# A hand-written order of 812 steps, searched anew: more matmuls on zeros ahead of the first transposes, and chunk 6 stored by SyncE

## The chip, the cores and the metric

The kernel runs on one core of a Trainium2 chip. The metric is the device time of the whole kernel in microseconds, the median of three runs. In the text TensorE is PE, VectorE is DVE, ScalarE is ACT, GpSimd is POOL and SyncE is SP, as in the profile; "PEld" is PE's weight load.

## What is computed

Linear attention with the feature map phi, and a feed-forward network with a product of two projections on its output:

```python
def phi(x):
    return np.where(x > 0, x, np.exp(x) - 1.0) + 1.0
q_p, k_p = (phi(q), phi(k))                    # q, k, v: (8 batches, 8 heads, 576, 64), f32
kv = np.einsum('bhsd,bhse->bhde', k_p, v)
z = np.sum(k_p, axis=2)
num = np.einsum('bhsd,bhde->bhse', q_p, kv)
den = np.einsum('bhsd,bhd->bhs', q_p, z)[..., None] + 1e-06
x = (num / den) ...                            # heads side by side: (4608, 512)
out = ((x @ w1) * (x @ w2) @ w3) @ w_out       # w1, w2: 512x1024; w3: 1024x1024; w_out: 1024x512
```

## The kernel before, in words

**Staging.** A batch has 576 rows: 512 of them make one chunk, and the 64 left over of all eight batches make a ninth chunk (number 8). The product w3 @ w_out is formed once (eight blocks of 128 rows), since the two matrices follow each other with nothing between them. Then for each batch: phi of k and q, the 64x64 state `kv` of each head, the numerator and denominator, the division, a transpose to `xt`, and for each chunk eight blocks `f` of the two projections, their product `ab`, and four output blocks `o`.

**The order.** Nothing is looped at run time. A string `ORDER` (L451 to L522) lists every step; the loop at L528 issues them one after the other, and each engine takes its own instructions in exactly that order. `GATES` (L523) adds six waits that hold loads back until another load has landed. A step is `name:arguments`; a letter at the end names the engine of a copy (`a` ACT, `v` DVE) or the queue of a transfer (`s` SP, `g` POOL).

The steps that the text speaks of:

- `const:i` (L94): memsets; `const:1` makes the identity `ident` for transposes, on POOL. `warm:n,i` (L110): n matmuls of 128x128 zeros that nothing reads.
- `l3` (L155), `lo` (L148), `lw` (L141): load the blocks of w3, w_out, w1 and w2 on POOL's queue, with a cast. `ld` (L117): 1 MB, or part of it, of one batch of q, k or v, into a pool of five buffers. `lr`, `lp` (L124, L132): the left-over rows of k, q or v of one batch or two.
- `w3t` (L352): eight transposes of a w3 block on PE; `w3c` (L359): its copy out of PSUM. `wa`, `wf` (L369, L378): the product with w_out; `wc` (L385): the copy into `wf_sb`.
- `x` (L164), `t` (L170), `m` (L177): phi of four heads (exp on ACT, max and add on DVE) and of a pair of heads (min on DVE). `xr`, `tr`, `mr` the same for the left-over rows.
- `v` (L216), `vr` (L222): the cast of v. `kv` (L230): the state of two heads, on PE; `kc`, `kh` (L246, L255): its copy out of PSUM.
- `qt` with `qc` (L262, L271), or `qd` (L277, an SP transfer): the transpose of q. `na` (L288): numerator and denominator, on PE; `nd` (L305): three DVE instructions that divide. `xp` with `xc` (L328, L337), or `xd` (L342, an SP transfer): the transpose into `xt`.
- `f` (L397), `fk` (L401): one block of a chunk in both projections, 8 matmuls; `fk` does part of the inner dimension. `ac` (L405): the copy of the first, on ACT; `ab` (L410): the product, on DVE. `o` (L415), `oc` (L422), `st` (L434): an output block, its copy, its store. `ol` (L439): the last output block, in two halves.

PSUM has four buffers for `f`, `o`, `qt`, `xp`, `w3t` and `warm` together (`mm_ps`, L61) and two for `kv`, `na` and `wa` (`at_ps`, L62). So the third `f` in a row starts only when the first one's `ac` and `ab` are done. `v` has one cast buffer (L66).

```python
    for s in ORDER.split():
        name, *args = s.split(":")
        made = steps[name](*(int(a) if a.isdigit() else a for a in (args[0].split(",") if args else ())))
        issued[s] = made
        if s in gates:
            tc.add_manual_dep(made.ins, issued[gates[s]].ins.name, ...)
```

Of the kernel before, what the change touches and what calls it, by code (L numbers as in the profile page):

```python
# [18 lines left out]
def kernel(  # L19
# [441 lines left out]
    kv:0,2 t:q,0,4,4 kc:0,0,1,1,a kh:0,2,1,a kv:0,3 kh:0,2,0,v ld:k,1,0,8,g m:q,0,4,2 na:0,0 kh:0,3,0,a
    w3t:6 kh:0,3,1,v m:q,0,4,3 na:0,1 nd:0,0 qt:0,2,2 ld:q,1,0,8,g w3t:7 w3c:6,v qc:0,2,2,a xp:0,0
    w3c:7,v wf:6 ld:v,1,0,4,g lr:k,1,s xc:0,0,a nd:0,1 lr:v,1,s ld:v,1,4,4,g na:0,3 xp:0,1 wc:6,v na:0,2
    wf:7 nd:0,3 xc:0,1,v nd:0,2 xp:0,3 fk:0,0,0,2 wc:7,v xc:0,3,a xp:0,2 xc:0,2,v fk:0,0,2,1 fk:0,0,3,1
    ac:0,0,a f:0,1 ab:0,0 xr:k,0,1 ac:0,1,a tr:k,0,1 mr:k,0,1 f:0,2 ab:0,1 ac:0,2,a f:0,5 ab:0,2 vr:1,v
    ac:0,5,a f:0,4 ab:0,5 ac:0,4,a t:k,1,0,4 x:k,1,4,4 f:0,6 t:k,1,4,4 x:k,1,0,4 ab:0,4 m:k,1,4,2
    ac:0,6,a f:0,7 m:k,1,0,0 m:k,1,0,1 ab:0,6 x:q,1,0,4 lp:k,1,s t:q,1,0,4 f:0,3 ac:0,7,a m:q,1,0,0
    ld:k,2,0,8,s m:q,1,0,1 v:1,0,4,a m:k,1,4,3 ab:0,7 ac:0,3,a kv:1,1 t:q,1,4,4 qt:1,0,2 x:q,1,4,4
    ab:0,3 kv:1,0 o:0,2 v:1,6,2,a kc:1,0,1,1,v lp:v,1,s m:q,1,4,3 qc:1,0,2,a m:q,1,4,2 kc:1,0,1,0,a
    v:1,4,2,a qt:1,2,2 oc:0,2,v na:1,1 ld:q,2,0,8,s kv:1,2 qc:1,2,2,a st:0,2,g nd:1,1 kv:1,3 o:0,3  # L470
    kh:1,2,1,a kh:1,3,0,a kh:1,3,1,v kh:1,2,0,v ld:v,2,0,8,s xp:1,1 x:k,2,0,4 t:k,2,4,4 na:1,2 na:1,0
    oc:0,3,v o:0,1 xr:k,1,2 nd:1,2 st:0,3,g x:k,2,4,4 ld:k,3,0,8,s nd:1,0 xc:1,1,a na:1,3 xp:1,2
    oc:0,1,a m:k,2,4,3 o:0,0 nd:1,3 xc:1,2,a st:0,1,g tr:k,1,2 vr:3,a t:k,2,0,4 xp:1,3 vr:2,a xp:1,0
    m:k,2,0,0 x:q,2,0,4 xc:1,3,v lp:k,2,s xc:1,0,v m:k,2,0,1 oc:0,0,a f:1,1 mr:k,1,2 x:q,2,4,4 m:k,2,4,2
    st:0,0,g t:q,2,0,4 ac:1,1,a m:q,2,0,0 f:1,4 m:q,2,0,1 ab:1,1 v:2,4,4,a t:q,2,4,4 ac:1,4,a f:1,0
    m:q,2,4,2 ld:q,3,0,8,s m:q,2,4,3 v:2,0,4,a ab:1,4 qd:2 ac:1,0,a kv:2,1 ab:1,0 kv:2,0 f:1,5 x:k,3,4,4
    t:k,3,0,4 t:k,3,4,4 ac:1,5,a f:1,2 x:k,3,0,4 ab:1,5 ac:1,2,a f:1,3 ab:1,2 ac:1,3,a kv:2,2 x:q,3,4,4
    tr:k,2,2 ld:v,3,0,8,s f:1,7 ab:1,3 xr:k,2,2 ac:1,7,a mr:k,2,2 lp:v,2,s f:1,6 ab:1,7 ac:1,6,a kv:2,3
    ab:1,6 o:1,3 ld:k,4,0,8,s kc:2,0,2,0,a kc:2,0,2,1,a m:k,3,4,2 m:k,3,0,1 m:k,3,4,3 m:k,3,0,0
    x:q,3,0,4 na:2,3 na:2,1 t:q,3,0,4 o:1,0 lp:q,0,s oc:1,3,a nd:2,1 v:3,4,4,a st:1,3,g nd:2,3 xp:2,1  # L480
    v:3,0,4,a o:1,1 m:q,3,0,1 ld:q,4,0,8,s xc:2,1,v oc:1,0,a m:q,3,0,0 t:q,3,4,4 st:1,0,g na:2,0
    m:q,3,4,2 oc:1,1,a na:2,2 m:q,3,4,3 xp:2,3 o:1,2 nd:2,0 st:1,1,g qd:3 x:k,4,0,4 nd:2,2 x:k,4,4,4
    t:k,4,4,4 xp:2,0 xp:2,2 xc:2,3,a kv:3,3 xc:2,0,v kv:3,2 xc:2,2,a oc:1,2,v kv:3,1 vr:4,a kv:3,0
    t:k,4,0,4 st:1,2,g f:2,0 kc:3,0,2,0,a m:k,4,0,0 vr:5,a m:k,4,0,1 kc:3,0,2,1,a m:k,4,4,3 ac:2,0,a
# [12 lines left out]
    kv:5,3 nar:0 kv:5,1 ab:4,6 f:3,6 kc:5,0,2,0,a m:k,6,4,3 vr:7,a kc:5,0,2,1,v m:k,6,4,2 ac:3,6,a
    m:k,6,0,0 m:k,6,0,1 na:5,2 ld:v,6,0,8,s f:3,1 ndr:0 nd:5,2 xdr:0 ac:3,1,a ab:3,6 na:5,0 na:5,1 f:4,7
    nd:5,0 nd:5,1 ac:4,7,a na:5,3 ab:3,1 ld:q,6,0,8,s f:4,4 nd:5,3 ld:k,7,0,8,s v:6,0,4,a ab:4,7 xd:5
    o:3,1 ac:4,4,a v:6,4,4,a ab:4,4 kv:6,1 oc:3,1,a o:3,0 st:3,1,g x:q,6,4,4 t:q,6,0,4 o:3,2 t:q,6,4,4  # L500
    oc:3,0,a m:q,6,4,3 x:q,6,0,4 m:q,6,4,2 st:3,0,g kv:6,0 oc:3,2,v kv:6,3 kv:6,2 x:k,7,0,4 ld:q,7,0,8,s
    m:q,6,0,0 o:3,3 st:3,2,g m:q,6,0,1 t:k,7,0,4 qd:6 kc:6,0,2,0,a kc:6,0,2,1,a x:k,7,4,4 m:k,7,0,1
    m:k,7,0,0 f:4,1 oc:3,3,v t:k,7,4,4 st:3,3,g ac:4,1,a m:k,7,4,2 f:4,2 m:k,7,4,3 ab:4,1 ac:4,2,a
    ab:4,2 f:5,5 ac:5,5,a o:4,0 ab:5,5 f:5,2 oc:4,0,v x:q,7,4,4 lp:q,1,s t:q,7,4,4 st:4,0,g ac:5,2,a
    t:q,7,0,4 x:q,7,0,4 f:5,3 ab:5,2 ac:5,3,a f:5,4 ab:5,3 ac:5,4,a m:q,7,0,1 lp:q,2,s m:q,7,4,3 na:6,3
    m:q,7,0,0 na:6,1 ab:5,4 o:4,1 lp:q,3,s nd:6,1 m:q,7,4,2 ld:v,7,0,8,s nd:6,3 f:5,0 qd:7 oc:4,1,v
    ac:5,0,a st:4,1,g na:6,0 o:4,2 ab:5,0 nd:6,0 o:4,3 oc:4,2,a st:4,2,g na:6,2 v:7,0,4,a f:5,7 tr:q,1,2
    nd:6,2 oc:4,3,a v:7,4,4,a xd:6 st:4,3,g kv:7,1 kv:7,0 ac:5,7,a f:5,1 xr:q,1,2 ab:5,7 ac:5,1,a
    mr:q,1,2 xr:q,2,2 tr:q,2,2 kv:7,3 ab:5,1 kv:7,2 f:5,6 kc:7,0,2,1,a kc:7,0,2,0,v qdr:1 mr:q,2,2
    ac:5,6,a tr:q,3,2 xr:q,3,2 na:7,3 qdr:2 na:7,0 ab:5,6 o:5,0 nd:7,0 nd:7,3 o:5,1 oc:5,0,a st:5,0,g  # L510
    f:6,1 oc:5,1,a st:5,1,g ac:6,1,a f:6,0 ab:6,1 ac:6,0,a na:7,1 f:6,3 ab:6,0 nd:7,1 ac:6,3,a o:5,3
    mr:q,3,2 ab:6,3 nar:5 oc:5,3,a nar:4 f:6,6 ndr:5 st:5,3,g ndr:4 ac:6,6,a nar:2 xdr:2 na:7,2 ab:6,6
    f:6,7 nd:7,2 ac:6,7,a ndr:2 xd:7 f:6,4 ab:6,7 ac:6,4,a o:5,2 ab:6,4 nar:3 oc:5,2,a f:6,5 qdr:3 ndr:3
    st:5,2,g ac:6,5,a xdr:1 f:6,2 ab:6,5 ac:6,2,a f:7,4 ab:6,2 ac:7,4,a f:7,0 ab:7,4 ac:7,0,a o:6,0
    ab:7,0 nar:7 oc:6,0,v nar:6 o:6,3 ndr:7 st:6,0,g ndr:6 f:7,7 oc:6,3,a xdr:3 st:6,3,g ac:7,7,a o:6,2
    ab:7,7 f:7,3 oc:6,2,v st:6,2,g ac:7,3,a f:7,6 ab:7,3 ac:7,6,a f:7,5 ab:7,6 ac:7,5,a f:7,2 ab:7,5
    ac:7,2,a f:8,5 ab:7,2 ac:8,5,a f:8,6 ab:8,5 ac:8,6,a f:8,3 ab:8,6 ac:8,3,a f:8,2 ab:8,3 ac:8,2,a
    f:8,1 ab:8,2 ac:8,1,a f:8,0 ab:8,1 ac:8,0,a f:8,4 ab:8,0 ac:8,4,a f:8,7 ab:8,4 ac:8,7,a o:6,1 ab:8,7
    o:8,2 oc:6,1,a st:6,1,g o:8,3 oc:8,2,a st:8,2,s o:8,0 oc:8,3,v st:8,3,s f:7,1 oc:8,0,a st:8,0,s
    ac:7,1,a o:8,1 ab:7,1 o:7,1 oc:8,1,v st:8,1,s o:7,2 oc:7,1,v st:7,1,s o:7,0 oc:7,2,a st:7,2,s ol:7,3  # L520
    oc:7,0,v st:7,0,s
    """  # L522
    GATES = "lp:k,1,s<ld:q,1,0,8,g ld:k,2,0,8,s<ld:q,1,0,8,g lp:v,1,s<ld:q,1,0,8,g ld:q,2,0,8,s<ld:q,1,0,8,g ld:v,2,0,8,s<ld:q,1,0,8,g lr:k,1,s<lw:0,0,256"  # L523
    ctx.enter_context(tc.manual_schedule())
    gates = dict(g.split("<") for g in GATES.split())

# [36 lines left out]
```

## Time and profile before

| what | us |
|---|---|
| runs | 255.71, 256.59, 256.50; median 256.5 |
| profiled execution, its own time | 255.47 |
| its span, first to last instruction | 253.3 |
| PE busy in the span | 238.3 (94%) |
| DVE, ACT, POOL busy | 165.0, 125.2, 37.4 |
| mean granted TensorE clock | 0.996 |
| first transposes on PE, start | 7.54 |
| first `f` with all of the inner dimension (`f:0,1`), start | 41.63 |
| last matmul, start of its group of 16 | 247.20 |
| a 128x512 matmul, start to start (8 of them: 1.73) | 0.216 |
| `ab` on DVE, `ac` on ACT, one each | 0.685, 0.584 |
| 1 MB load on SP's queue, issue to landing (median of k, q, v) | 8.8, 8.8, 6.9 |
| store of a block on POOL's queue, on SP's, issue to landing (median) | 5.1, 2.4 |

How to read it: "busy" is the time in which an engine had an instruction running. Matmuls are pipelined, so the durations shown for single ones (379 ns for 512 columns) overlap; the distance from one start to the next is what counts. A row of the timeline gives the start, the length, the engine, the line, the tiles and the number of instructions merged, and in brackets the idle time before and what ended it. "SPq" and "POOLq" are instructions that only issue a transfer; the time to landing is counted from their start.

### The profile page before, as it was taken

To read this page: it belongs to the slowest core of one execution; us is meant where nothing else is said; L and a number is where in the kernel's file an instruction comes from. 1 tells how busy PE (TensorE), PEld (TensorE's weight loads), DVE (VectorE), ACT (ScalarE), POOL (GpSimd) and SP (SyncE) were. 2 spreads that over 40 slices of the span, in tenths; PEclk is the share of its full clock that TensorE was granted. 3 is DMA by queue.
4 is the path that set the end of the run, shared out by engine and by line. 5 is a ranking of instruction groups with operands and counts; after the bars stand their busy time and mean duration, and the time that the engine had idled before them with its cause. 6 is when DMAs were issued, how large, how long until landed. Compare 5 with 4: busy or idle time off the path is not lost.

```text
span 253.3 us, 4047 instructions
## 1 busy us (share of the span) xinstructions
PE 238.3 (94%) x1498; PEld 126.7 (50%) x1498; DVE 165.0 (65%) x364; ACT 125.2 (49%) x190; POOL 37.4 (15%) x63
## 2 busy tenths in 40 slices
PE   4899689999899999999999999999999999999993
PEld 4845654456345554544445454445454444444442
DVE  7405787799965997997877975866467454343131
ACT  3327723698976876822665684437332322333200
POOL 8654710002100200011000020110100011000000
PEclk9999999999999999999999999999999999999998
DMA  6999999999999999999993999999406413000543
GB/s 124 201 274 346 204 199 309 300 244 337 301 238 274 304 246 317 198 183 299 259 285 112 278 290 265 216 259 159 112 21 116 115 43 104 3 0 0 128 121 124
DMA packets 69363, 50.06 MB, mean 198 GB/s; under 512 B 41312, under 2 KB 64096, under 8 KB 69344
## 3 DMA queue, kind: packets, MB, share of 16 engines
q1 hardware_dynamic: 59840, 30.81, 54.9%
q0 software_dynamic: 9360, 18.88, 28.0%
q8 instruction: 11, 0.18, 0.3%
q10 hardware_dynamic: 144, 0.13, 0.2%
q14 instruction: 8, 0.07, 0.1%
HBM read 38.80 MB, written 9.44 MB: 190 GB/s over the span
## 4 chain that ended last, share of the span: by engine, by line
PE 71%; DVE 16%; ACT 5%; issue 4%; POOL 2%; DVEq 0%; ACTq 0%; POOLq 0%
PE a_ps L393 20%; PE b_ps L393 20%; PE o_ps L418 19%; DVE xn L299 3%; PE wa L373 3%; ACT e L166 2%; PE kvp L238 2%; DVE t L172 2%; DVE ab L412 2%; PE w3p L356 2%; DVE k L180 1%; DVE r L298 1%; DVE q L180 1%; PE nd L291 1%; PE warm L113 1%
## 5 line engine op out<-in xcount | busy, mean ns | idle before, releaser
L393 PEld LDWEIGHTS <-w_sb 128*128 128x128 bf16 x576 | 55.4, 98 | 64.9 <-DVE xt L338 1.4
L412 DVE TENSOR_TENSOR ab<-a_sb,b_ps 128x512 bf16<-128x512 f32 x72 | 49.2, 685 | 42.0 <-PE b_ps L393 37.2
L407 ACT COPY a_sb<-a_ps 128x512 f32<-128x512 f32 x72 | 42.0, 584 | 66.4 <-PE a_ps L393 64.6
L393 PE MATMUL a_ps<-xt,w_sb 128*128 128x512 bf16 x256 | 66.0, 379 | 1.8 <-DVE xt L338 1.8
L393 PE MATMUL b_ps<-xt,w_sb 128*128 128x512 bf16 x256 | 66.0, 379 | 0.0
L418 PE MATMUL o_ps<-wf_sb,ab 128*128 128x512 bf16 x280 | 64.9, 379 | 0.1
L436 POOL DMA_DIRECT2D out_dram<-o_sb x28 | 15.7, 559 | 186.2 <-ACT o_sb L424 105.1
L418 PEld LDWEIGHTS <-ab 128*128 128x128 bf16 x280 | 26.6, 98 | 29.6 <-DVE ab L412 0.9
L424 ACT COPY o_sb<-o_ps 128x512 f32<-128x512 f32 x18 | 10.5, 584 | 27.6 <-PE o_ps L418 27.6
L299 DVE TENSOR_TENSOR xn<-nd,r 128x512 bf16<-128x512 f32 x32 | 22.1, 692 | 1.1
L424 DVE COPY o_sb<-o_ps 128x512 f32<-128x512 f32 x17 | 11.7, 688 | 11.2 <-PE o_ps L418 11.2
L166 ACT ACTIVATE e<-q 128x1024 bf16<-128x1024 f32 x16 | 16.9, 1060 | 1.5 <-DVE k L180 1.2
L166 ACT ACTIVATE e<-k 128x1024 bf16<-128x1024 f32 x16 | 16.6, 1054 | 0.4 <-DMA k<-in_k_dram 0.3
L172 DVE TENSOR_SCALAR t<-k 128x1024 bf16<-128x1024 f32 x16 | 10.7, 689 | 8.6 <-DMA k<-in_k_dram 8.6
L217 ACT CAST vt<-v 128x1024 bf16<-128x1024 f32 (+1 forms) x15 | 14.3, 970 | 0.0
L180 DVE TENSOR_TENSOR k<-t,e 128x512 bf16<-128x512 bf16 x32 | 12.1, 421 | 2.8 <-ACT e L166 2.4
L238 PE MATMUL kvp<-vt,k 128*128 128x130 bf16 x128 | 11.1, 220 | 2.3 <-DVE kvb L248 1.8
L180 DVE TENSOR_TENSOR q<-t,e 128x512 bf16<-128x512 bf16 x32 | 12.3, 420 | 0.7 <-ACT e L166 0.3
L291 PE MATMUL nd<-kvb,qt 128*128 128x130 bf16 x128 | 11.4, 220 | 1.0 <-DVE xn L299 0.6
L291 PEld LDWEIGHTS <-qt 128*128 128x128 bf16 x128 | 8.9, 98 | 5.5 <-DVE xn L299 0.7
L238 PEld LDWEIGHTS <-k 128*128 128x128 bf16 x128 | 9.1, 98 | 5.1 <-issue 1.5
L172 DVE TENSOR_SCALAR t<-q 128x1024 bf16<-128x1024 f32 x16 | 10.7, 687 | 0.4 <-DMA q<-in_q_dram 0.4
(69 smaller groups left out, 196.0 us busy)
## 6 DMA issues: line engine op xcount, KB each, us to landing
out_dram<-o_sb POOLq DMA_DIRECT2D x28, 256.0 KB, 5.1
k<-in_k_dram SPq DMA_DIRECT2D x6, 1024.0 KB, 8.8
q<-in_q_dram SPq DMA_DIRECT2D x6, 1024.0 KB, 8.8
v<-in_v_dram SPq DMA_DIRECT2D x6, 1024.0 KB, 6.9
w3b<-in_moe_w_dram POOLq DMA_DIRECT2D x8, 256.0 KB, 8.2
v<-in_v_dram POOLq DMA_DIRECT2D x3, 512.0 KB, 18.5
out_dram<-o_sb SPq DMA_DIRECT2D x9, 128.0 KB, 2.3
k32r<-in_k_dram SPq DMA_DIRECT2D x8, 128.0 KB, 10.0
```

The costliest lines, as they stand in the source:

```text
L166: return nc.scalar.activation(out=e[:, 0:nh * W], in_=raw[n, b][:, h0 * W:(h0 + nh) * W], func=AF.Exp)
L172: nc.vector.tensor_scalar(out=d[:, 0:nh * W], in0=raw[n, b][:, h0 * W:(h0 + nh) * W], scalar1=0.0, scalar2=1.0, op0=ALU.max, op1=ALU.add)
L180: nc.vector.tensor_tensor(out=d[:, hp].rearrange("p j u d -> p u j d"), in0=ts[n, b, h0][:, s].rearrange("p (u j d) -> p u j d", u=2, j=NJ ...
L238: nc.tensor.matmul(dst, kj[:, hp, j].rearrange("p u d -> p (u d)"), vt[:, j, 2 * hp:2 * hp + 2, :].rearrange("p h e -> p (h e)"), start=(j ...
L291: nc.tensor.matmul(o[:, j // 2, (j % 2) * 256:(j % 2) * 256 + PW], sb["qt", b][:, hp, j * P:(j + 1) * P], kvb[b][:, hp].rearrange("p u e - ...
L299: nc.vector.tensor_tensor(out=dst, in0=o[:, :, :, 0:D], in1=r.unsqueeze(3).to_broadcast(list(r.shape) + [D]), op=ALU.mult)
L393: nc.tensor.matmul(o, w[:, kc, f * P:(f + 1) * P], xt_of(c)[:, :, kc, :], start=(kc == 0), stop=(kc == KC - 1))
L407: return copy_of[eng](out=d, in_=ps["a", c, f])
L412: nc.vector.tensor_mul(out=d[:, f, :], in0=sb["a", c, f], in1=ps["b", c, f])
L418: nc.tensor.matmul(d, sb["ab", c][:, f, m * P:(m + 1) * P], wf_sb[:, f, :], start=(f == 0), stop=(f == FC - 1))
L424: return copy_of[eng](out=d, in_=ps["o", c, m])
L436: queue_of[queue].dma_start(out=dst, in_=sb["o", c, m][r])
```

## The change

Only `ORDER` and `GATES` change. Both strings have the same 812 steps but for these: `warm:18,9` is new (18 matmuls on zeros), `warm:10,13` is gone (10 of them); some 60 copies out of PSUM, casts and stores carry another letter, among them the four stores of chunk 6, which go from POOL's queue to SP's. Everything else is order. GATES holds the same six pairs. The core of the diff, with the places that the text speaks of:

```diff
     ORDER = """
-    const:0 const:2 lr:k,0,s const:9 l3:0 lr:v,0,s const:11 l3:1 warm:26,0 const:3 l3:2 l3:3 lo:0,2
-    xr:k,0,0 const:6 lo:2,2 const:8 const:7 lo:4,2 zr:0,1 tr:k,0,0 lo:6,2 mr:k,0,0 const:10 l3:4 const:4
-    const:1 l3:5 zr:0,0 const:5 w3t:0 ld:k,0,0,4,g warm:8,1 w3c:0,a w3t:1 warm:8,2 w3c:1,v vr:0,a
...
-    wa:7,1 l3:7 t:k,0,0,4 w3c:4,a wf:5 wc:2,v wc:3,a wc:1,v lw:0,0,256 wc:0,a t:k,0,4,4 x:k,0,0,4 wf:4
-    lw:1,0,256 wc:5,a m:k,0,0,0 m:k,0,0,1 x:q,0,0,4 warm:10,10 t:q,0,0,4 wc:4,a warm:10,11 lw:0,1,256
-    m:q,0,0,1 x:q,0,4,4 m:q,0,0,0 warm:10,12 warm:10,13 x:k,0,4,4 lw:1,1,256 v:0,0,4,v qt:0,0,2
-    m:k,0,4,3 lw:0,1,512 kv:0,1 qc:0,0,2,a m:k,0,4,2 kv:0,0 v:0,4,2,v lw:1,1,512 kc:0,0,1,0,v v:0,6,2,a
-    kv:0,2 t:q,0,4,4 kc:0,0,1,1,a kh:0,2,1,a kv:0,3 kh:0,2,0,v ld:k,1,0,8,g m:q,0,4,2 na:0,0 kh:0,3,0,a
-    w3t:6 kh:0,3,1,v m:q,0,4,3 na:0,1 nd:0,0 qt:0,2,2 ld:q,1,0,8,g w3t:7 w3c:6,v qc:0,2,2,a xp:0,0
-    w3c:7,v wf:6 ld:v,1,0,4,g lr:k,1,s xc:0,0,a nd:0,1 lr:v,1,s ld:v,1,4,4,g na:0,3 xp:0,1 wc:6,v na:0,2
...
+    const:0 const:5 lr:k,0,s l3:0 const:6 lr:v,0,s l3:1 const:3 warm:26,0 l3:2 const:1 l3:3 xr:k,0,0
+    const:11 lo:0,2 const:2 const:4 lo:2,2 tr:k,0,0 warm:18,9 mr:k,0,0 lo:4,2 const:8 lo:6,2 const:7
+    w3t:0 const:9 warm:8,1 l3:4 w3c:0,a zr:0,0 w3t:1 l3:5 const:10 warm:8,2 zr:0,1 w3c:1,a ld:k,0,0,4,g
...
+    w3c:4,v l3:6 w3t:5 wc:1,a wc:3,v wf:4 w3c:5,a wc:0,v l3:7 t:k,0,0,4 x:k,0,0,4 wc:2,v warm:10,10
+    wc:4,v lw:0,0,256 wf:5 x:k,0,4,4 m:k,0,0,0 m:k,0,0,1 t:k,0,4,4 lw:1,0,256 x:q,0,0,4 warm:10,11
+    m:k,0,4,2 wc:5,v warm:10,12 t:q,0,0,4 lw:0,1,256 x:q,0,4,4 m:q,0,0,1 m:q,0,0,0 m:k,0,4,3 qt:0,0,2
+    t:q,0,4,4 lw:1,1,256 qc:0,0,2,a m:q,0,4,3 lw:0,1,512 m:q,0,4,2 v:0,0,4,v v:0,4,2,a qt:0,2,2
+    lw:1,1,512 v:0,6,2,a kv:0,2 kv:0,1 qc:0,2,2,a kh:0,2,1,v kv:0,3 ld:k,1,0,8,g w3t:6 kh:0,3,1,v
+    kh:0,3,0,v kh:0,2,0,a kv:0,0 w3c:6,a na:0,3 kc:0,0,1,1,v ld:q,1,0,8,g w3t:7 kc:0,0,1,0,v nd:0,3
+    na:0,0 wf:6 w3c:7,a nd:0,0 ld:v,1,0,4,g lr:k,1,s lr:v,1,s xp:0,3 na:0,1 ld:v,1,4,4,g wc:6,a na:0,2
...
+    oc:0,1,v xp:1,1 na:1,0 o:0,2 v:2,0,4,a nd:1,2 st:0,1,g ld:v,3,0,8,s vr:3,a nd:1,0 xc:1,1,a na:1,3
+    o:0,0 oc:0,2,a nd:1,3 st:0,2,g xr:k,1,2 tr:k,1,2 xp:1,3 oc:0,0,v xp:1,0 x:q,2,0,4 xp:1,2
+    ld:k,3,0,8,s t:q,2,4,4 st:0,0,g xc:1,3,a t:q,2,0,4 xc:1,0,a m:q,2,0,0 xc:1,2,a m:q,2,0,1 mr:k,1,2
...
-    m:q,2,4,2 ld:q,3,0,8,s m:q,2,4,3 v:2,0,4,a ab:1,4 qd:2 ac:1,0,a kv:2,1 ab:1,0 kv:2,0 f:1,5 x:k,3,4,4
-    t:k,3,0,4 t:k,3,4,4 ac:1,5,a f:1,2 x:k,3,0,4 ab:1,5 ac:1,2,a f:1,3 ab:1,2 ac:1,3,a kv:2,2 x:q,3,4,4
...
+    ab:1,0 f:1,1 ac:1,1,a f:1,2 ab:1,1 x:k,3,4,4 t:k,3,4,4 ld:q,3,0,8,s t:k,3,0,4 kv:2,2 x:k,3,0,4
+    kv:2,1 f:1,5 kc:2,0,2,0,v lp:k,2,s m:k,3,4,3 kc:2,0,2,1,a m:k,3,0,0 ac:1,2,a m:k,3,4,2 ac:1,5,a
+    ab:1,2 f:1,3 v:3,0,4,a ab:1,5 m:k,3,0,1 lp:v,2,s ac:1,3,a v:3,4,4,a na:2,0 kv:3,1 ab:1,3 kv:3,0
...
-    ab:7,0 nar:7 oc:6,0,v nar:6 o:6,3 ndr:7 st:6,0,g ndr:6 f:7,7 oc:6,3,a xdr:3 st:6,3,g ac:7,7,a o:6,2
-    ab:7,7 f:7,3 oc:6,2,v st:6,2,g ac:7,3,a f:7,6 ab:7,3 ac:7,6,a f:7,5 ab:7,6 ac:7,5,a f:7,2 ab:7,5
...
+    o:6,2 nd:7,0 nd:7,2 o:6,3 oc:6,2,a st:6,2,s o:6,0 oc:6,3,a st:6,3,s o:6,1 oc:6,0,v st:6,0,s na:7,1
+    oc:6,1,v na:7,3 nd:7,1 st:6,1,s f:8,4 nd:7,3 ac:8,4,a f:8,5 xd:7 ab:8,4 ac:8,5,a f:8,6 ab:8,5
+    ac:8,6,a f:8,2 ab:8,6 ac:8,2,a f:8,7 ab:8,2 ac:8,7,a f:7,0 ab:8,7 ac:7,0,a f:7,3 ab:7,0 ac:7,3,a
...
     """
```

The loads on SP's queue after the start stand in this order. Before: left-over k, `ld:k,2`, left-over v, `ld:q,2`, `ld:v,2`, `ld:k,3`, left-over k, `ld:q,3`, `qd:2`, `ld:v,3`. After: left-over v, `ld:v,2`, left-over k, `ld:q,2`, `ld:k,2`, `ld:v,3`, `ld:k,3`, `qd:2`, `ld:q,3`.

## The prediction

> **What bounds the kernel now.** I read the page first: busy shares, then the slices of PE and of the DMA engines.
>
> ```profile
> PE 238.3 (94%) x1498; PEld 126.7 (50%) x1498; DVE 165.0 (65%) x364; ACT 125.2 (49%) x190; POOL 37.4 (15%) x63
> ...
> PE   4899689999899999999999999999999999999993
> ...
> DMA  6999999999999999999993999999406413000543
> ```
>
> PE has holes in its first six slices (a slice is 6.33 us) and few afterwards. The DMA row matters as much: the 16 engines are 9 in every slice from 6 to 133 us. Second view: what PE waited for.
>
> ```profile
> PE w3p L356 <- POOL ident masks.py:199: 3.4, 1, 3.4
> PE kvp L238 <- DVE kvb L248: 1.8, 1, 1.8
> PE a_ps L393 <- DVE xt L338: 1.8, 2, 1.3
> ...
> PE xtp L333 <- DVE xn L299: 0.9, 2, 0.6
> PE nd L291 <- DVE xn L299: 0.6, 1, 0.6
> ```
>
> Third, PE's timeline, to see when. From `f:0,1` at 41.63 on PE waits four times: 1.26, 0.58, 0.55 and 0.17 = 2.56 us. So a new order can gain nearly all of its time only ahead of 41.63.
>
> ```profile
> 7.54 1.01 PE L356 MATMUL w3p<-ident,w3b 128*128 128x128 bf16 x8 [3.39 <-POOL ident masks.py:199]
> 30.11 0.39 PE L238 MATMUL kvp<-vt,k 128*128 128x130 bf16 x4 [1.82 <-DVE kvb L248]
> 41.63 1.03 PE L393 MATMUL a_ps<-xt,w_sb 128*128 128x512 bf16 x4
> 66.09 1.04 PE L393 MATMUL a_ps<-xt,w_sb 128*128 128x512 bf16 x4 [1.26 <-DVE xt L338]
> ```
>
> Fourth, the landings of the 1 MB loads on SP's queue (issue plus time to landing, asked for one load at a time): k2 56.7, q2 61.0, v2 65.2, k3 71.1, q3 75.7; v1 ended at 52.1. ACT's timeline shows that k3's exp starts as k3 lands; here PE is not late for it, since `kv:3` comes at 90.5.
>
> ```profile
> 71.11 1.06 ACT L166 ACTIVATE e<-k 128x1024 bf16<-128x1024 f32 x1
> ```
>
> **What the Trainium skill says.** "TensorE: Matmul & The Clock Gate", Part 1: the array runs at half rate until a free-running window of about 3.4 us has been busy throughout. The trace agrees: from 7.54 the transposes and zeros start 107 ns apart, from 12.45 on 56 ns. "Perfetto Trace Analysis", Per-engine timelines: ACT and DVE are strict FIFO, so an exp that waits for a load holds every copy behind it. The trace's ACT and DVE do keep the written order. "DMA: Bandwidth & Descriptors", Issuing engines are not separate DMA queues: transfers of SP and POOL share 16 engines. The trace doesn't separate this for stores: 5.1 us to landing from POOL, 2.4 from SP, at different load.
>
> **Part by part. The zeros.** 18 more at 107 ns move their end from 3.98 to 5.91. The identity moves ahead on POOL (from 7.49 to about 3.6), the first w3 block lands at 5.2: the first transposes start at 5.9, not 7.54, perhaps at full clock already. Both are hidden: the `wa` products wait for w_out, whose four parts land at 11.2, 12.5, 13.8 and 15.0, and POOL's queue keeps its order, so k, q, v of batch 0 land as before (19.6 to 27.1). If the clock stays low, four groups of eight at 0.85 instead of 0.45 us (1.6 us) fall into the same slack. Taken: 0, bounds -0.3 and +0.5.
>
> **The first batch.** Before, w3t copies (1.28 us) and wc copies (0.69, 0.60) stand between the divisions on DVE, and `kv:0,2` waits for a late exp (k's second half landed at 21.2, its exp ran at 27.23). After, the exps of k follow their landing and ACT takes these copies. Laid end to end: `wa` from 11.2, eight times 0.86 and one w3 block of 0.45, ends at 18.55. DVE then, by the durations of its groups less the overlap of neighbours: wc:3, wc:0 to 19.95; t:k (k landed at 19.6) to 20.6; wc:2, wc:4 to 22.0; two min of 0.38 to 22.8; the second t:k (landed at 21.2) and a min to 23.9; wc:5 to 24.55; t:q to 25.2; three min to 26.4; the second t:q and two min to 27.85; the cast of v 0.69, to 28.55. ACT keeps ahead of it: its exps run at 20.2, 21.3, 22.7 and 24.2, each 1.06. Then four `kv` of 0.28 with four copies of 0.22 between (a `kv` waits for the copy before it, as at 30.11) to 30.8; two `kc` to 31.5; four divisions of 1.15 (0.16+0.20+0.69 and two hand-overs) to 36.45; last `xp` 36.8; the last two `xc` on ACT 0.58 each to 37.85; a quarter of the inner dimension is 0.43. `f:0,2` starts at 39.05. Gain here: 41.63-39.05 = 2.6, from 1.5 to 3.5.
>
> **From there on.** The remaining PE work is the same in both orders: 71 `f` and 35 `o` of 1.727, `ol` 1.77, 28 `kv` of 0.283, 28 `na` of 0.227, eight `nar` of 0.235, eight `xp` of 0.223, two `qt` of 0.446: 203.7 us. Before: 41.63+203.7 = 245.3, and the last matmul ends at 247.20+1.77 = 248.97: 3.65 lost, 2.56 in the four waits, 1.1 in changes between shapes. After, without a wait: 39.05+203.7 = 242.75.
>
> **What is late next.** Data doesn't come 2.6 us sooner: the transfers were saturated. (1) v1's first half is cast after two exps of q1 (landed at 48.16; two `ac` and an exp of k stand before them, so they run at 49.2 and 50.2), at 51.2 to 52.25; `kv:1,0`, else at 51.6, waits for it: 0.7, and `o:0,3` and the other `kv:1` behind it. (2) The copies `xc:1,3`, `xc:1,0`, `xc:1,2` stand behind `x:q,2,0,4` on ACT, which waits for q2, second on SP's queue as before, 61.0: exp to 62.1, copies to 63.7, so `f:1,6` at 63.2 where it would be at 62.6: 0.6 more, and 0.4 at `f:1,1`, whose buffers come free behind two exps of k2 (about 64.7). (3) k3 is now the fifth load behind v1, not the fourth. Fifth before was q3 at 75.7; from the other side 71.1 plus 1.05 MB at the 299 GB/s of this stretch (3.5 us) is 74.6. I take 74.6, bounds 72 and 77. `x:k,3,4,4`, `x:k,3,0,4` (2.0) and `kc` (0.38) stand ahead of `ac:1,2` (0.58) on ACT, and both `t:k,3` ahead of `ab:1,2` on DVE. `f:1,3` needs the PSUM buffers of `f:1,2`, so it starts at 74.6+3.05 = 77.7; without waits it stood at 73.4. All waits up to there sum to 4.3, 2.6 of them here. Queued behind: `ac:1,5`, `v:3`, `ac:1,3`, and through them `kv:3` and `f:1,4`. Later loads have slack: q3 about 80, needed about 81; k4 about 88, needed at 91.
>
> **Letters.** Some 60 copies and casts change between ACT (0.584 for 128x512) and DVE (0.688). Ahead of 39 us this is counted above; behind, PE has at most 0.1 us of it per copy on its path, of either sign. Taken 0.
>
> **Stores of chunk 6.** Four issues of 0.5 us move to SP, ahead of `xd:7`. It needs `nd:7,3`, about 2.9 us after `na:7,3`, and transposes took 4.6 to 8.1 us to land; `f:7,0` comes 8.9 us after. Hidden, or up to 2 late. Taken 0. POOL, freed of them, has nothing else to do. The tail (`ol`, its copies and stores) is the same: last matmul to end of span 253.3-248.97 = 4.3.
>
> **The sum.** 77.7 plus the work behind it (242.75-73.4 = 169.4), 0.9 for changes of shape, 1.0 for waits (before: 0.58+0.55+0.17 = 1.3 in this part) is 249.0, against 248.97. Span 253.3, the profiled execution 255.5; the median of the runs stands 1.0 above that execution: 256.5.
>
> **The rivals.** *A, likeliest (0.40):* the start gains 2.6 and the loads take it back: 256.5, own range 255.2 to 257.8. That zeros or clock don't do what they should belongs here too, since that part is hidden. *B, faster (0.27):* the loads of batches 2 and 3 come sooner, k3 at 72: `f:1,3` at 75.1, 2.6 less, 253.9. For it: 60 to 66 us carried 331 GB/s with stores among it. Against: all 9s in the DMA row, and 12 to 15 us from issue to landing for v2, k3 and q3. *C, slower (0.33):* k3 lands later still, and ACT and DVE, with its exp and max at their heads, hold the copies that free PSUM for `f:1,3`. Four stores of chunk 0 and the transposing `qd:2` share the engines with k3; each us past 74.6 is a us of PE. From 75.9 on it decides; at 77.2 the time is 259.1. For it: `kv:3` comes 11 us sooner on PE than before (79.6, not 90.5), on loads that do not; against: only 1 MB more lies ahead of k3.
>
> **How the numbers follow.** 0.5% is 1.28 us, about what a measurement of this kernel can tell from no change. Faster by more: B, 0.27; within: A, 0.40; slower: C, 0.33. The range leaves out about 0.1 on each side: 253.2 (k3 near 71.5 and no later wait) to 260.0 (k3 at 77, or at 76 with `xd:7` late by 2).
>
> **What would show it.** First transposes at 5.9; `f:0,2` at 39.05; `xc:1,3` on ACT right behind an exp that starts at 61; k3's exp at 74.6, PE idle two to three us before `f:1,3` near 77.7, ended by `ac` or `ab`. Wrong, if k3's exp starts at 72 or sooner, if `f:0,2` starts after 41, or if new waits of over 2 us stand behind 80.

## The result and the profile after

The changed kernel takes 256.13 us (median of 18 runs, 254.60 to 258.91), the kernel before 255.30 us (18 runs beside them, 254.30 to 256.59). The ratio is 1.0019, with a 95% interval of 0.9995 to 1.0043: no difference that can be measured. The profiled execution took 255.72 us, its span is 254.0. A few executions took over 1.5% longer than the fastest of their kernel (one of these 18 runs and one run each in four of the experiments, with the stores on POOL the profiled one); they are in the medians and ranges, but not in the ratios, and their traces are left out.

The page's busy shares and slices of the changed kernel, as shown of before:

```profile
PE 236.7 (93%) x1490; PEld 125.6 (49%) x1506; DVE 165.8 (65%) x372; ACT 123.5 (49%) x182; POOL 35.3 (14%) x59
...
PE   8798699989798999999999999999997999999993
...
DMA  6999999999999999999999996907496435000165
```

PE's first slice has gone from 4 to 8: before, PE waited there for the identity, now it also runs 18 more matmuls on zeros there. In return the eleventh slice (63 to 70 us) is a 7 where it was an 8, and the 31st (190 to 197 us) a 7 where it was a 9. The DMA row is 9 in every slice from 6 to 152 us; before, the row of 9s broke at 133. What PE waited for (us in total, times, longest):

```profile
PE qtp L267 <- DVE q L180: 3.3, 3, 1.5
PE a_ps L393 <- ACT xt L338: 2.4, 2, 1.9
PE b_ps L393 <- ACT a_sb L407: 1.9, 1, 1.9
...
PE w3p L356 <- DMA w3b<-in_moe_w_dram: 1.1, 2, 0.6
PE a_ps L393 <- ACT a_sb L407: 0.9, 1, 0.9
```

The 3.4 us for the identity are gone. Of the 3.3 in the first row two waits, 1.48 and 1.18, fall in the start (26.02 and 27.82), and the third, 0.60, at 52.10. PE's timeline says when the rest comes; the rows are the first transposes, `f:0,2`, `f:1,6`, `f:1,3`, and the second half of `f:6,5`:

```profile
5.73 0.61 PE L356 MATMUL w3p<-ident,w3b 128*128 128x128 bf16 x8
...
39.26 1.03 PE L393 MATMUL a_ps<-xt,w_sb 128*128 128x512 bf16 x4
...
64.95 1.08 PE L393 MATMUL a_ps<-xt,w_sb 128*128 128x512 bf16 x4 [1.94 <-ACT xt L338]
...
77.58 1.02 PE L393 MATMUL a_ps<-xt,w_sb 128*128 128x512 bf16 x4 [0.92 <-ACT a_sb L407]
...
193.05 1.02 PE L393 MATMUL b_ps<-xt,w_sb 128*128 128x512 bf16 x4 [1.89 <-ACT a_sb L407]
```

PE enters the projections 2.37 us sooner than before (41.63), and loses 5.81 us in waits from there on (the three in brackets, 0.60 at 52.10, 0.25 at 89.11 and 0.21 at 131.34) where it lost 2.56 before. It should come out 2.37 - (5.81 - 2.56) = -0.88, later by 0.88, and it does: its last group of 16 starts at 248.06, 0.86 later than before (247.20). Who is late is read one step further back, on ACT's timeline. Three exps wait for a load (the bracket), and the copies that PE needs are the rows behind them:

```profile
62.88 1.06 ACT L166 ACTIVATE e<-q 128x1024 bf16<-128x1024 f32 x1 [0.76 <-DMA q<-in_q_dram]
63.85 1.54 ACT L338 COPY xt<-xtp 128x512 bf16<-128x512 bf16 x3
...
74.52 2.00 ACT L166 ACTIVATE e<-k 128x1024 bf16<-128x1024 f32 x2 [2.12 <-DMA k<-in_k_dram]
76.55 0.37 ACT L248 CAST kvb<-kvp 64x260 bf16<-64x260 f32 x1
76.95 1.07 ACT L407 COPY a_sb<-a_ps 128x512 f32<-128x512 f32 x2
...
190.52 2.00 ACT L166 ACTIVATE e<-q 128x1024 bf16<-128x1024 f32 x2 [4.16 <-DMA q<-in_q_dram]
192.43 0.57 ACT L407 COPY a_sb<-a_ps 128x512 f32<-128x512 f32 x1
```

These are q2, k3 and q7. The first two were forecast; q7 was not. Before, `ld:q,7` was issued at 147.76 and landed at 156.4; the new order issues it at 181.66, and it lands at 190.5, with `ac:6,3` behind its exp.

### The profile page after: what moved, and what is told of

The parts are those of the page before. It is cut to its first block, busy times and chain, and to the rows that moved or that the text cites. A ratio compares the mean times of both kernels' runs of the same rounds, so it can differ in the third digit from the quotient of the medians.

```text
span 254.0 us, 4055 instructions
## 1 busy us (share of the span) xinstructions
PE 236.7 (93%) x1490; PEld 125.6 (49%) x1506; DVE 165.8 (65%) x372; ACT 123.5 (49%) x182; POOL 35.3 (14%) x59
## 4 chain that ended last, share of the span: by engine, by line
issue 55%; PE 22%; DMA 14%; POOL 6%; ACT 1%; POOLq 0%; ACTq 0%
PE o_ps L418 7%; PE b_ps L393 7%; PE a_ps L393 6%; POOL out_dram L436 5%; DMA q<-in_q_dram 4%; DMA w_sb<-in_moe_w_dram 4%; DMA wo<-in_moe_w_out_dram 3%; DMA out_dram<-o_sb 3%; POOL w3b L159 1%; PE o_ps L445 1%; ACT e L166 0%; PE nd L291 0%; PE kvp L238 0%; POOL wo L151 0%; ACT a_sb L407 0%
## 5 line engine op out<-in xcount | busy, mean ns | idle before, releaser
L418 PE MATMUL o_ps<-wf_sb,ab 128*128 128x512 bf16 x267 | 62.2, 379 | 0.7
L436 POOL DMA_DIRECT2D out_dram<-o_sb x24 | 13.8, 574 | 147.2 <-ACT o_sb L424 93.5
L424 ACT COPY o_sb<-o_ps 128x512 f32<-128x512 f32 x22 | 12.9, 585 | 23.8 <-PE o_ps L418 23.7
L424 DVE COPY o_sb<-o_ps 128x512 f32<-128x512 f32 x13 | 8.9, 688 | 14.6 <-PE o_ps L418 14.5
```

The costliest lines, as they stand in the source:

```text
L418: nc.tensor.matmul(d, sb["ab", c][:, f, m * P:(m + 1) * P], wf_sb[:, f, :], start=(f == 0), stop=(f == FC - 1))
L424: return copy_of[eng](out=d, in_=ps["o", c, m])
L436: queue_of[queue].dma_start(out=dst, in_=sb["o", c, m][r])
```

## The experiments

The **theory**: a load at the head of ACT's and DVE's queues (k3 above all, q7 later) sets PE's time, and takes back what the start gains. The **rivals**: the start's gain reaches the end and something else loses it; the waits add up, so that each one removed is a gain; the stores or the zeros are to blame.

### q7 sooner

```diff
-t:k,7,0,4 x:k,7,0,4 qdr:2 m:k,7,4,3
+t:k,7,0,4 x:k,7,0,4 qdr:2 ld:q,7,0,8,s ld:v,7,0,8,s m:k,7,4,3
-oc:5,1,a qdr:3 st:5,1,g ac:6,0,a ld:q,7,0,8,s o:5,3 ab:6,0 o:5,2 ld:v,7,0,8,s oc:5,3,a
+oc:5,1,a qdr:3 st:5,1,g ac:6,0,a o:5,3 ab:6,0 o:5,2 oc:5,3,a
```

> The changed kernel, with the loads of q7 and v7 put 12 steps of SyncE's queue sooner (right behind qdr:2, issue near 161 instead of 181.7). In the changed kernel's trace PE waits 1.89 us at 193.05, because ac:6,3 on ScalarE stands behind the exps of q7, which landed at 190.50. Theory (a late transfer at the head of a queue is what PE loses): q7 lands before 180, that wait is gone, the span falls from 254.0 to about 252.1, ratio to the kernel before about 0.995. Rival (the time is lost elsewhere or the wait hides another, such as the divisions of batch 7 or the cast of v7): the wait moves to another place behind 190 and the span stays within 0.5 of 254.0.

254.15 us (22 runs), ratio 0.9947 (0.9928 to 0.9965), span 252.6. q7 lands at 169.8, and ACT runs its exp at 187.04 without waiting for it:

```profile
187.04 2.01 ACT L166 ACTIVATE e<-q 128x1024 bf16<-128x1024 f32 x2
188.94 0.57 ACT L407 COPY a_sb<-a_ps 128x512 f32<-128x512 f32 x1
```

PE has no wait behind 132.12. So the late place of q7 (v7 was moved with it) is what makes the change a draw: without it the new order is 0.5% faster than before, and the two intervals do not meet (0.9928 to 0.9965 here, 0.9995 to 1.0043 for the changed kernel).

### The exps of q2 and k3 behind the copies they hold

```diff
-xp:1,0 x:q,2,0,4 xp:1,2 ld:k,3,0,8,s t:q,2,4,4 st:0,0,g xc:1,3,a t:q,2,0,4 xc:1,0,a m:q,2,0,0 xc:1,2,a
+xp:1,0 xp:1,2 ld:k,3,0,8,s t:q,2,4,4 st:0,0,g xc:1,3,a t:q,2,0,4 xc:1,0,a xc:1,2,a x:q,2,0,4 m:q,2,0,0
```

> The changed kernel, with the exp of q2 on ScalarE put behind the three copies xc:1,3, xc:1,0, xc:1,2 that it held up. In the changed kernel's trace PE waits 1.94 us for them at 64.95. Theory (k3 sets the time of f:1,3, whatever PE does ahead of it): f:1,6 starts near 63.0, f:1,3 still at 77.4 to 77.8 with a wait in front of it that has grown from 0.92 to 2.5 or more, no change of the span (253.5 to 254.3). Rival (the waits add up): f:1,3 near 75.7, span near 252.1.

256.70 us, ratio 1.0044 (1.0020 to 1.0068), span 253.4. `f:1,6` starts at 64.42, `f:1,3` at 77.40 with 0.86 in front of it: no gain, and 252.1 is ruled out. The wait of 2.5 that the theory expected did not come either: PE entered the projections 0.70 later in this execution (39.96), so there was less to take back. And the test says little of q2 itself, which landed at 61.0 here, not at 62.8. `f:1,6` still waits 0.71, and 0.71 or 0.72 in each of the other profiled experiments on the new order: so it seems that 0.7 is the path from the transposes through three copies, and that q2 added 1.2 of the 1.94 in the one execution.

```diff
-ab:1,1 x:k,3,4,4 t:k,3,4,4 ld:q,3,0,8,s t:k,3,0,4 kv:2,2 x:k,3,0,4 kv:2,1 f:1,5 ...
+ab:1,1 ld:q,3,0,8,s kv:2,2 kv:2,1 f:1,5 ... ac:1,2,a ac:1,5,a x:k,3,4,4 x:k,3,0,4
+ab:1,2 f:1,3 v:3,0,4,a ab:1,5 t:k,3,4,4 t:k,3,0,4 m:k,3,4,3 m:k,3,0,0 m:k,3,4,2 m:k,3,0,1
```

> The changed kernel, with the exps of k3 on ScalarE put behind ac:1,2 and ac:1,5, and its max and min on VectorE behind ab:1,2 and ab:1,5. Theory: f:1,3 no longer waits for k3 and starts at 76.7 instead of 77.58, 0.9 sooner; kv:3,1 behind it then comes at 78.4 and finds the min of k3 done (78.0). What is gained is given back by the next load, q3, which landed at 80.84 and stands ahead of ac:1,4: o:1,0 starts no sooner than 82.5 (83.06 in the changed kernel), so the span falls by 0 to 0.6. Rival (only k3's place held PE): the whole 0.9 is kept, span 253.1.

257.08 us, ratio 1.0052 (1.0031 to 1.0073), span 254.2. `f:1,3` starts at 76.38 without a wait, but the min of k3 ends at 80.16, not 78.0, and PE waits for it one step later:

```profile
80.21 0.40 PE L238 MATMUL kvp<-vt,k 128*128 128x130 bf16 x4 [1.72 <-DVE k L180]
```

So the gain was given back, but not to q3, as the expectation had it: the exps of k3 now run 2.2 us later (76.67 instead of 74.52), and its own min is late. All three edits together, with two steps of `kv:3` one block later:

```diff
-ab:1,2 f:1,3 ... na:2,0 kv:3,1 ab:1,3 kv:3,0 f:1,4 nd:2,0
+ab:1,2 f:1,3 ... na:2,0 ab:1,3 f:1,4 kv:3,1 kv:3,0 nd:2,0
```

> The changed kernel with all three: q7 and v7 sooner, exp of q2 behind the copies, exps of k3 behind ac:1,5 (with kv:3,1 and kv:3,0 behind f:1,4). Theory (the loads of batches 2 to 4 are the bound up to about 90, so a wait that is taken away there comes back at the next load): f:1,3 near 75, but o:1,0 at 82.4 to 83.0, as ac:1,4 stands behind the exp of q3 (landed 80.84); of the 2.9 us ahead of it 0.1 to 0.7 are kept, and 1.9 at 193: span 251.4 to 252.1. Rival (the waits add up): span 249.2 to 249.6.

254.68 us, ratio 0.9982 (0.9960 to 1.0003), span 252.4; `f:1,3` at 76.66, `o:1,0` at 83.44, with a new wait of 0.97 for a division at 82.20. With all three edits the kernel is no faster than with q7 alone (0.9947). That these waits add up is ruled out, since the span would be 249.2 to 249.6: what was taken from k3 came back within 6 us.

### PE later at the start

Matmuls on zeros put in front of the projections delay PE, while the loads keep their places. In the changed kernel 43 are put in, in the kernel with q7 sooner 22:

```diff
-xc:0,0,a xc:0,2,a fk:0,0,0,2
+xc:0,0,a xc:0,2,a warm:43,13 fk:0,0,0,2
...
-xc:0,0,a xc:0,2,a fk:0,0,0,2
+xc:0,0,a xc:0,2,a warm:22,13 fk:0,0,0,2
```

> The changed kernel, with 43 more matmuls on zeros (2.4 us of PE) right in front of the first block of the projections (fk:0,0,0,2), so that PE loses there again what the new start had gained; loads, exps and copies stand where they stood. Theory (the loads of batches 1 to 3 take the start's gain back): q1 and v1 (51 to 53), q2 (61 to 63) and k3 (74.3 to 75.2) land as before; f:0,2 starts near 42, but the wait of 0.6 at 52 and that of 0.9 in front of f:1,3 take most of it up: f:1,3 at 77.4 to 78.4; the span grows by 0.2 to 0.9, ratio to the kernel before 1.003 to 1.006. Rival (the start's gain reaches the end, and something else lost it): span +2.4, ratio near 1.011.

> The kernel with q7 and v7 sooner (ratio 0.9947), and 22 more matmuls on zeros (1.2 us of PE) in front of the first block of the projections. Theory (k3 takes back about the last microsecond of what the start gains, no more): the wait of 0.9 to 1.3 in front of f:1,3 falls to 0 to 0.3 and f:1,3 starts within 0.3 of 78.0; ratio 0.995 to 0.9965. Rival (the whole delay goes through to the end): ratio near 0.9995.

With 22: 253.71 us, ratio 0.9934 (0.9914 to 0.9954): no loss against 0.9947, though `f:0,2` came 1.7 us later. ACT still waited for k3, but PE no longer did (`f:1,3` has no bracket):

```profile
74.17 2.00 ACT L166 ACTIVATE e<-k 128x1024 bf16<-128x1024 f32 x2 [0.43 <-DMA k<-in_k_dram]
```

```profile
77.84 1.03 PE L393 MATMUL a_ps<-xt,w_sb 128*128 128x512 bf16 x4
```

With 43: 259.24 us, ratio 1.0151 (1.0107 to 1.0196), more than either side expected. Six executions side by side explain the first half of that. (k3's landing is the start of the exp that waited for it, less 0.02; with 43 zeros no exp waited, and it is the issue plus the time to landing.)

| execution | `f:0,2` | k3's landing | `f:1,3` | its wait |
|---|---|---|---|---|
| changed kernel | 39.26 | 74.50 | 77.58 | 0.92 |
| exp of q2 behind | 39.96 | 74.32 | 77.40 | 0.86 |
| q7 sooner | 40.12 | 75.20 | 78.28 | 1.34 |
| without 18 zeros (below) | 41.74 | 73.82 | 77.75 | 0 |
| q7 sooner, 22 zeros | 41.83 | 74.15 | 77.84 | 0 |
| 43 zeros | 43.02 | 74.6 | 79.03 | 0 |

In the last three, `f:1,3` comes 36.0 after `f:0,2`; in the first three it comes 3.08 after k3's landing, whatever PE did. It is the later of the two, and with k3 at 74.5 they meet at 41.6 (77.58 - 36.0). So **in this order a start of the projections sooner than about 41.6 is worth nothing at `f:1,3`, and before, it stood at 41.63.** (k3 landed between 73.8 and 75.2 in these executions; that puts the meeting point between 40.9 and 42.3.)

This also says that the 0.5% left with q7 sooner does not come from the start. With 22 zeros PE enters the projections at 41.83, no sooner than before, and the kernel is 0.7% faster than before all the same. From there to its last group of 16 (245.95) it takes 204.12 us, the kernel before 205.57. The waits on this way sum to 1.56 instead of 2.56. Before, behind the 1.26 at 66.09:

```profile
90.27 0.40 PE L333 MATMUL xtp<-ident,xn 128*128 128x128 bf16 x4 [0.58 <-DVE xn L299]
...
139.04 0.40 PE L291 MATMUL nd<-kvb,qt 128*128 128x130 bf16 x4 [0.55 <-DVE xn L299]
...
191.01 0.40 PE L291 MATMUL nd<-kvb,qt 128*128 128x130 bf16 x4 [0.17 <-DVE xnr L299]
```

With q7 sooner and 22 zeros, all of them:

```profile
54.67 0.62 PE L267 MATMUL qtp<-ident,q 128*128 128x128 bf16 x8 [0.59 <-DVE q L180]
...
66.30 1.08 PE L393 MATMUL a_ps<-xt,w_sb 128*128 128x512 bf16 x4 [0.71 <-ACT xt L338]
...
89.38 0.62 PE L333 MATMUL xtp<-ident,xn 128*128 128x128 bf16 x8 [0.26 <-DVE xn L299]
```

So by these two traces most of what is kept is shorter waits in the middle of the order. Which of its steps shortened them was not tried.

The second half of the loss with 43 zeros is in part a feedback. SP's queue holds transposing transfers that wait for PE's results, with loads behind them. With 43 zeros k5 was issued at 116.71, 1.04 later than in the changed kernel (115.67), and landed at 129.13 instead of 125.73. So PE, 1.5 us late, became late by nearly another 2 us. Only the 1.04 follow from PE's delay through the queue: the load also took 12.4 us instead of 10.1, and why is not shown.

```profile
129.15 2.00 ACT L166 ACTIVATE e<-k 128x1024 bf16<-128x1024 f32 x2 [2.21 <-DMA k<-in_k_dram]
131.66 0.69 DVE L412 TENSOR_TENSOR ab<-a_sb,b_ps 128x512 bf16<-128x512 f32 x1 [2.17 <-ACT a_sb L407]
132.41 1.47 PE L418 MATMUL o_ps<-wf_sb,ab 128*128 128x512 bf16 x6 [1.11 <-DVE ab L412]
...
134.75 0.40 PE L238 MATMUL kvp<-vt,k 128*128 128x130 bf16 x4 [0.87 <-DVE k L180]
```

### The zeros, left out and alone

```diff
-lo:2,2 tr:k,0,0 warm:18,9 mr:k,0,0
+lo:2,2 tr:k,0,0 mr:k,0,0
```

> The changed kernel without warm:18,9. Theory (the products wa wait for w_out, whose parts land by POOL's queue): the first transposes still start near 5.2 to 5.8, perhaps 107 ns apart instead of 56, the first wa still near 11.3, f:0,2 within 0.4 of 39.3 to 40, no change of the time: ratio 1.000 to 1.004. Rival (the zeros keep the clock up through the start and that is worth time): transposes and wa at half rate, f:0,2 later by 1 or more, ratio 1.006 or more.

> The kernel with q7 and v7 sooner (ratio 0.9947), without warm:18,9. Theory (in front of f:0 the zeros are hidden behind the landing of w_out): ratio 0.993 to 0.996. Rival (without the zeros a stretch of the start runs at half rate, as 28 to 34 us did in the first execution without them): f:0,2 later by 1 to 2 us, half of it kept to the end: ratio 0.997 or more.

Out of the changed kernel: 255.95 us, ratio 1.0044 (1.0016 to 1.0073). Out of the one with q7 sooner: 255.36 us, 0.9987 (0.9963 to 1.0011), against 0.9947. The intervals of each pair touch or overlap, in the second pair just so. `f:0,2` starts at 41.74 and 42.07, against 39.26 to 40.37 in seven profiled executions of the new order with the zeros and no added delay. The start of the second kernel without zeros:

```profile
5.16 1.04 PE L356 MATMUL w3p<-ident,w3b 128*128 128x128 bf16 x8 [1.01 <-DMA w3b<-in_moe_w_dram]
...
8.02 1.03 PE L356 MATMUL w3p<-ident,w3b 128*128 128x128 bf16 x8 [0.98 <-DMA w3b<-in_moe_w_dram]
...
11.41 1.06 PE L356 MATMUL w3p<-ident,w3b 128*128 128x128 bf16 x8
12.27 1.06 PE L113 MATMUL warm<-zero 128*128 128x128 bf16 x8
13.12 6.34 PE L373 MATMUL wa<-wo,w3A 128*128 128x512 bf16 x28
```

Eight transposes take 0.85 us there, from start to start of the next group, instead of 0.45, and `wa` starts at 13.12, not 11.45 to 12.44, and without a wait for w_out. So in this execution the missing zeros are not hidden. In the first kernel without them `wa` started at 11.85, no later than with them, and PE ran at half rate from 28.2 to 34 instead. That stretch is no sure sign of the missing zeros: the clock granted from 30 to 34 us was 0.50 there and 0.57 in the second kernel without them, but also 0.58 with 43 zeros, 0.68 with 22 and 0.71 with the exps of k3 behind, and all three have `warm:18,9`. In the rest it was 1.00, and a group of eight transposes has a length of 0.61 there, not the 1.06 that it has at half rate.

Nor is the later start what costs time at the end. With 22 zeros in front of the projections `f:0,2` starts only 0.24 sooner than in the second kernel without zeros, and the time is 1.65 us less (0.9934 against 0.9987, intervals apart). In the traces these two differ most in a wait of 1.45 at 178.26 for `xd:6`, whose transfer landed at 178.2 behind v7 (174.1). Why it came late there stays open.

The other way round, the zeros and the sooner identity alone, in the old order:

```diff
-warm:26,0 const:3 l3:2 l3:3 lo:0,2 ... const:1 l3:5 zr:0,0 const:5 w3t:0
+warm:26,0 const:3 l3:2 const:1 l3:3 lo:0,2 ... l3:5 zr:0,0 const:5 warm:18,9 w3t:0
```

> The kernel before, with one part of the change alone: the identity sooner on POOL's queue (behind l3:1) and the 18 matmuls on zeros in front of the first transposes. Theory: the first transposes start at 5.7 to 6, wa at 11.5 to 12.2 instead of 13.44, but the first batch behind it is bound by its own exps, copies and divisions in the old order: f:0,1 between 40.3 and 41.6 (before: 41.63), of which the wait at 66 takes half: ratio 0.996 to 1.000. Rival (the start's gain is that of wa, the new order of the first batch adds nothing): f:0,1 near 39.8, ratio 0.993 to 0.995.

255.15 us, ratio 0.9984 (0.9970 to 0.9999), span 253.8. `f:0,1` starts at 39.92, 1.71 sooner than before: the rival's number for the start, so the two edits together bring most of what the whole new order of the start brings (2.37). The ratio is the theory's. PE holds its lead up to 88, loses most of it at 108, to the next load that it runs into, and starts its last group of 16 at 247.76, 0.56 later than before:

```profile
105.77 1.06 ACT L166 ACTIVATE e<-k 128x1024 bf16<-128x1024 f32 x1 [1.85 <-DMA k<-in_k_dram]
...
108.08 2.12 PE L418 MATMUL o_ps<-wf_sb,ab 128*128 128x512 bf16 x9 [1.55 <-DVE ab L412]
```

This k5 landed at 105.75 here and at 105.06 before: the 1.7 us that PE was ahead did not make it sooner.

### The stores of chunk 6 on POOL again

```diff
-oc:6,2,a st:6,2,s o:6,0 oc:6,3,a st:6,3,s o:6,1 oc:6,0,v st:6,0,s ... st:6,1,s
+oc:6,2,a st:6,2,g o:6,0 oc:6,3,a st:6,3,g o:6,1 oc:6,0,v st:6,0,g ... st:6,1,g
```

> The changed kernel with the four stores of chunk 6 back on POOL's queue. Theory: xd:7 waits for the divisions of batch 7, not for the four issues (about 0.5 us each) ahead of it on SyncE, so it is issued within 0.3 of 210.9, no wait of PE behind 195 in either kernel; ratio 1.000 to 1.004. Rival (the stores on SyncE hold xd:7, or the slower landing on POOL reaches the end): a change of 0.5 us or more of either sign.

256.37 us, ratio 1.0041 (1.0020 to 1.0062), against 1.0019 (0.9995 to 1.0043): the intervals overlap, so no effect of the stores is shown; one of about 0.5 us is not ruled out. In the changed kernel the last store of chunk 6 is issued at 208.82 and `xd:7` at 210.88, 1.7 us after that store has left the queue, and PE waits for nothing there. When `xd:7` is issued in the variant is not shown.

### k3 ahead of v3, and one order on DVE

```diff
-nd:1,2 st:0,1,g ld:v,3,0,8,s vr:3,a ... xp:1,2 ld:k,3,0,8,s
+nd:1,2 st:0,1,g vr:3,a ... xp:1,2 ld:k,3,0,8,s ld:v,3,0,8,s
```

> The kernel with q7 and v7 sooner (ratio 0.9947), and k3 loaded ahead of v3 on SyncE's queue. Theory: k3 lands near 70.8, v3 near 74.6; the wait of 0.9 to 1.3 in front of f:1,3 is gone and v3 stands ahead of no copy that PE needs; q3 (about 81) is the next load that PE comes to, in front of ac:1,4, and gives part of it back: 0.2 to 0.7 sooner than without, ratio 0.992 to 0.994. Rivals: all of it is kept (0.990 to 0.991); or kv:3,1 waits for the cast of v3 instead and nothing is gained (0.995 or more).

253.62 us (6 runs), ratio 0.9931 (0.9906 to 0.9956), span 250.6. k3 landed at 70.1, v3 at 74.0, `f:1,3` started at 76.02 (36.0 after `f:0,2`), and the next load, q3, cost 0.32. The interval overlaps that of q7 sooner alone (0.9928 to 0.9965), so the time does not show a gain, though the wait at `f:1,3` is gone:

```profile
82.63 1.04 PE L418 MATMUL o_ps<-wf_sb,ab 128*128 128x512 bf16 x4 [0.32 <-DVE ab L412]
```

```diff
-f:0,4 m:k,1,4,2 ab:0,6 x:q,1,4,4 ld:v,2,0,8,s t:q,1,0,4 v:1,0,4,a
+f:0,4 m:k,1,4,2 t:q,1,0,4 ab:0,6 x:q,1,4,4 ld:v,2,0,8,s v:1,0,4,a
```

> The kernel with q7 and v7 sooner and k3 ahead of v3 (ratio 0.9931), and the max of q1 (t:q,1,0,4) put ahead of ab:0,6 on VectorE. Theory (the wait of 0.59 in front of qt:1,0,2 near 53 comes from VectorE's order, ab, max and two min behind each other in the time of one f block, not from a landing: it was 0.59 in five of the executions, with PE up to 3.8 us apart): it shrinks to 0 to 0.1, f:1,6 starts near 63.9 instead of 64.47; the next loads give some of it back, ratio 0.991 to 0.993. Rivals: q1 lands too late for that, and VectorE holds ab:0,6 for it, no gain or a loss (0.993 or more); all of it is kept (0.9908).

253.40 us (7 runs), ratio 0.9912 (0.9880 to 0.9945): the lowest ratio of all, though not to be told apart from the one before it, nor clearly from q7 sooner alone. The wait in front of `qt:1,0,2` fell from 0.59 to 0.28. PE came to q3 sooner, q3 came later (81.08), and the wait there grew:

```profile
81.10 1.06 ACT L166 ACTIVATE e<-q 128x1024 bf16<-128x1024 f32 x1 [2.63 <-DMA q<-in_q_dram]
...
83.41 1.04 PE L418 MATMUL o_ps<-wf_sb,ab 128*128 128x512 bf16 x4 [1.44 <-DVE ab L412]
```

## Why the prediction was right, and where its terms were off

**The mechanism** of the likeliest case, that the start gains and the loads take it back, is shown by the table of six executions and by the delay of 1.7 us that cost nothing. **That the time came out even is in part luck.** With q7 and v7 moved the ratio is 0.9947; on the 256.5 of the forecast that is 255.1, at the lower edge of the likeliest case's own range, 255.2 to 257.8. The 1.89 us at q7, which the prediction did not see, moved the time back to where it was forecast. One of its own signs of being wrong, new waits of over 2 us behind 80, came true with that, if it is meant as a sum: 1.89 and 0.21 stand at places where there was no wait before. The other two did not: k3's exp started at 74.52, and `f:0,2` at 39.26. PE's wait in front of `f:1,3` was 0.92, not two to three.

**The start**: `f:0,2` at 39.05 forecast, 39.26 measured; first transposes at 5.9 and 5.73. The sum was right and its parts were not. The zeros and the identity were put at 0, "hidden" by w_out; alone, in the old order, they bring 1.71. The working had them in it unseen: it let `wa` start at 11.2, as the loads allow, while before it started at 13.44 because the transposes began at 7.54 and ran at half rate. That the 1.6 us of half rate would fall into the slack in front of w_out was the wrong step: `wa` at 13.12 without a wait for w_out shows one execution that had no such slack. So the reordered first batch is worth about 0.7 at most, not 2.6 (39.92 to 39.26), and perhaps nothing: in six other executions with the zeros `f:0,2` came at 39.80 to 40.37, so 39.26, so close to the forecast, was the earliest of the seven.

**(1) v1's cast, 0.7.** PE waited 0.60, but at `qt:1,0,2` and for DVE's order. It was 0.59 or 0.60 in nine executions whose PE stood up to 3.8 us apart, and 0.28 with one step moved. With q7 sooner it was 1.25: there ACT had first waited 1.59 us for the left-over rows of v (their cast starts at 46.80), with a copy for PE and the exps of k1 and q1 behind it, which is the likely cause.

**(2) q2.** Forecast at 61.0, landed at 62.8; `f:1,6` at 64.95 instead of 63.2. In the later runs q2 came between 60.8 and 62.2. It cost nothing that k3 had not set already.

**(3) k3**, the step that the time hung on: 74.6 forecast, 74.50 measured; `f:1,3` 3.05 and 3.08 behind it, 77.7 and 77.58. Only the division among the waits was off: 2.6 were forecast in front of `f:1,3` and 0.92 came, because PE got there 1.56 later than forecast (76.66 instead of 75.1), 0.94 of it at q2.

**(4) What is behind it.** 1.0 forecast for later waits, 2.35 came (0.25, 0.21, 1.89). The prediction followed the loads up to k4 and put the rest under "Later loads have slack". q7 had lost its slack: its load was issued 34 us later. Less change between shapes than the 0.9 allowed gave back 0.4, and the last matmul ended at 249.83 instead of 249.0, the span at 254.0 instead of 253.3.

**Letters and stores**: the stores show no change that the runs can tell; the letters were not tried on their own. **The median** was put 1.0 above the profiled execution after three runs; it was 0.4 above it, and the kernel before came out at 255.3 in more runs. So 256.5 against 256.13 says less than the ratio: no change was forecast, and none is measured. **The range**: its upper end, 260.0 for "k3 at 77", does not follow from the prediction's own sum, which gives 258.9 (2.4 us later than 74.6).

## What to carry to other kernels

Where transfers are saturated, ask of each step that comes sooner which load it will run into: the step's time is the later of "work up to here" and "landing plus the chain behind it", and where the late exp was moved behind the copies, as here for k3, the wait only moved. Follow every moved load to the end of the order, not only those near the change. Work that looks hidden behind a load (here transposes at half rate) is hidden only if its own end, laid beside the landing, says so. And a gain seen in one stretch is not the gain at the end: delay that stretch on purpose and see what is left.

## What the runs showed of the hardware that was not expected

The transposing transfer `qd:2` held SP's queue for 7.04 us (67.21 to 74.25), with the load of q3 behind it, which was issued at 74.35 and landed at 80.84; `qd:7` held it for 2.04 at 193.36. A load of 1 MB took 8.8 us from issue to landing at 181.66, although the DMA engines had been only 13% busy from 176 to 181.6: on its way, with the load of v7 and three stores beside it, they were 79 to 96% busy. So transfers ahead of a load are not the only ones that make it late. The start of one order varied between executions: `wa` began at 11.45 to 12.44, as w_out landed. And PE fell to half rate without a long pause: with the exps of k3 behind, after waits of 1.47 and 1.18 us (26.34 and 28.15), from about 29 on. The changed kernel has the same two waits, 1.48 and 1.18, and kept its full rate there. The granted clock of the profile does not always show half rate: it is 1.00 from 4 to 12 us in the second kernel without zeros, while eight transposes take 0.85 instead of 0.45.
